# Attention over a cached context: K of some units scored ahead of a row's chain, V alone beside it, twelve chunks a row kept instead of eleven

## The chip, the cores and the metric

The kernel runs on one core of one Trainium2 chip. The metric is the device time of one execution in microseconds; the time before is the median of three runs. PE is the matrix engine, DVE the vector engine, ACT the scalar engine, POOL the general engine; SP's queue issues nearly all transfers.

## The reference

A batch of 8 rows, one token each, goes twice through an attention block and an MLP block. The attention reads the same cache of 4096 positions both times: 8 heads of K and V of 256 elements per row, 2 query heads on each. Cut to what matters:

```python
def _A_ref(x, k_cache, v_cache, wq, wo):          # x: (8, 1, 448)
    q = (x @ wq) as (B, 16 heads, 1, 256)
    scores = einsum("bhqd,bhkd->bhqk", q, k) * 256**-0.5
    o = einsum("bhqk,bhkd->bhqd", softmax(scores), v)
    return o as (B, 1, 4096) @ wo

x = x + _A_ref(_layernorm(x), K, V, wq, wo)
x = x + _B_ref(_layernorm(x), w1, w2, w3, w4)
x = x + _A_ref(_layernorm(x), K, V, wq, wo)
x = x + _B_ref(_layernorm(x), w1, w2, w3, w4)
```

With one token a row the shifted branch of `_B_ref` (w1, w2) adds nothing, since every shifted part is padding. What is left of it is `x + gelu(layernorm(x) @ w3) @ w4`. The cache is 268 MB, and the second pass over it needs a query that depends on the row's whole first pass.

## The kernel before

**Units and chunks.** Work is cut into units (pass, row, pair of heads), 2 x 8 x 4 of them. A unit has 4 chunks of K and 4 of V, each 1 MiB (128 partitions of 8 KB). Chunks live in 15 places in SBUF (`NC`, `slots`). `tasks` is the order of the units, `items` the order of the chunks: K chunk by chunk with V of the unit before between them (`due`). `loads` are the items that are fetched, in the same order; `emit_loads` (L660 to L707) issues a load on SP's queue, at L675 for two neighbouring places at once (2 MiB) and at L700 for one, whenever a place is free in program order. The issue then waits on the chip until the last reader of that place is done.

**K.** `transpose_k` (L713) turns a chunk on DVE in three instructions. `scores` (L728) multiplies it with the spread query `qbd`, 128 columns wide, or 256 wide when two chunks lie in neighbouring places; `paired` says which units are scored two chunks at a time. `exps` (L737) takes the exponential on ACT and its sums. `transpose_p` (L764, L771) turns the unit's p into `ptw`, from which `pv` (L783) multiplies a chunk of V in 16 products into a bank `o`.

**The row's chain.** After the last unit of a row's first pass, a serial chain runs: `half` (normalise and evict one bank, L420 to L467), output projection (`add_cols`, L358), `norm` (L220 to L298, with a power on POOL, L247), `mlp_hidden` (L376, GELU L394 to L399), w4 (L358), `norm` again, `project_q` (L309), which gives the query of the second pass; `spread_q` (L328, L332) lays it out. `chain`, `first_half`, `first_last` and `last` are Python generators. Each `yield` ends a step, and `step` puts steps into the engines' program before and after an item, so many that a given number (`total`) is spread over a given stretch of items. PE runs its program in order, so a step's products stand between the products of the chunks.

**What is kept.** `kept` names the chunks of a row that stay in their places from the first pass to the second: K of pairs 3 and 2, V chunks 1 to 3 of pair 3, 11 in all. `inner`, one more V chunk, is copied to PSUM (`away`, L748) and back (`back`, L755); a quarter of `part` goes to a fifth bank (L960, L978). While a row's chain runs, its 11 kept chunks hold 11 of the 15 places. Beside it stand three units with K and V: one or two of the second pass of the row before, and one or two of the first pass of a later row.

Of the kernel before, what the change touches and what calls it, by code (L numbers as in the profile page):

```python
# [17 lines left out]
def kernel(  # L18
# [42 lines left out]
    NC = 15  # L61

    kept = [(gp, 0, n) for gp in (GP - 1, GP - 2) for n in range(4)]
    kept += [(GP - 1, 1, n) for n in range(1, 4)]
# [45 lines left out]
    ptz = consts.tile([128, 520], BF16, name="ptw")  # L110
    nc.vector.memset(ptz[:], 0.0)
    ptw = ptz[:, 0:512].rearrange("p (a n w) -> p a n w", a=4, w=8)

    misc = psum.tile([128, 512], FP32, name="misc")
    ot_bank = misc[:, 256:320]
# [5 lines left out]
    nc.tensor.matmul(o_both[:], ptz[:, 0:128], ptz[:, 0:512], start=True, stop=True)  # L121

    def room_ps(what, nb):

        at, n = {"y": (320, 8), "st": (336, 2), "h": (352, HC), "q": (384, NB2)}[what]
        if nb == 1:
            return misc[:, at : at + n]
        if nb < Bn:
            at = {"y": 416, "st": 456, "h": 128}[what]
            return misc[:, at : at + n * nb]  # L130
        at, n = {"y": (0, 8), "st": (64, 2), "h": (80, HC), "q": (256, NB2)}[what]
        return store[0][:, at : at + n * nb]
# [40 lines left out]
    qbds = [consts.tile([128, 8, GP, 4, 2], BF16, name=f"qbd{k}") for k in range(3)]  # L173
# [127 lines left out]
    def project_q(b0, nb, qT):  # L301

        yield from norm(xT[:, :, b0 : b0 + nb], nb, False)
        q_ps = room_ps("q", nb).rearrange("p (c b) -> p c b", b=nb)
        for j in range(2):
            for h in range(Hq):
                for fc in range(4):
                    w, xi = wblk(wq_sb, HD, 2 * h + j, fc)
                    nc.tensor.matmul(  # L309
                        q_ps[:, j * Hq + h, :],  # L310
                        w,
                        xbs(nb)[:, xi, :],
                        start=(fc == 0),
                        stop=(fc == 3),
                    )
                if h % 4 == 3:
                    yield
        nc.vector.tensor_copy(qT, q_ps)
        yield
# [49 lines left out]
    def mlp_hidden(b0, nb):  # L369
# [3 lines left out]
        for c in range(HC):  # L373
            for fc in range(4):
                w, xi = wblk(w3_sb, F, c, fc)
                nc.tensor.matmul(  # L376
                    h_ps[:, c * nb : c * nb + nb],
                    w,
                    xbs(nb)[:, xi, :],
                    start=(fc == 0),  # L380
                    stop=(fc == 3),
                )
            if c % 4 == 3:
                yield
        yield
# [24 lines left out]
    def mlp(b0, nb):  # L410
        HT = yield from mlp_hidden(b0, nb)
        yield from out_cols(lambda c: HT[:, c, :], w4_sb, HC, b0, nb, 1)

    def z_cols(zall, gps):
# [15 lines left out]
        z_ps = misc[:, 480 : 480 + 4 * np_].rearrange("p (n g) -> p n g", n=4)  # L430
# [13 lines left out]

    def half(o_ps, zall, g8, OT):


# [7 lines left out]
        )  # L455
        o_sb = chn.tile([128, Dh], FP32, tag="o_sb")
# [4 lines left out]
        ot_ps = ot_bank[:, 32 * g8 : 32 * g8 + 16].rearrange("p (j h) -> p j h", j=2)  # L461
# [5 lines left out]
        nc.vector.tensor_copy(OT[:, :, 8 * g8 : 8 * g8 + 8], ot_ps)  # L467
        yield

    in_use = []  # L470

    def first_half(b, st):

        OT = work.tile([128, 2, Hq, 1], BF16, tag="OT", bufs=1)
        st["OT"] = OT
        yield from half(st["o", 0], st["z"], 0, OT[:, :, :, 0])
        yield from add_cols(
            y_room(1)[:, 0], lambda i: OT[:, i % 2, i // 2], wo_sb, range(NB2 // 2), 1
# [4 lines left out]
    def chain(b, st):  # L483
        OT = st["OT"]
        yield from half(st["o", 1], st["z"], 1, OT[:, :, :, 0])
        yield from add_cols(
            y_room(1)[:, 1], lambda i: OT[:, i % 2, i // 2], wo_sb, range(NB2 // 2, NB2), 1
# [8 lines left out]
    def first_last(b, st):  # L496

        yield from half(st["o", 1], st["z"], 1, OT2[:, :, :, b])
# [14 lines left out]
    def last(b, st):  # L513
        yield from half(st["o", 0], st["z"], 0, OT2[:, :, :, b])
# [13 lines left out]
    tasks = [(0, 0, gp) for gp in free + keep] + [(0, 1, gp) for gp in free]  # L528


    tasks += [(0, 2, free[0])]
    for b in range(Bn):
        tasks += [(1, b, gp) for gp in keep[::-1]]
        if b == Bn - 2:
            tasks += [(0, b + 1, gp) for gp in keep]
            tasks += [(1, Bn - 3, free[-1])] + [(1, b, gp) for gp in free]
        elif b == Bn - 1:
            tasks += [(1, b, gp) for gp in free]
        else:
            early = 0 < b < Bn - 3  # L540
            tasks += [(1, b, free[0])] * early + [(0, b + 1, gp) for gp in keep]
            tasks += [(1, b, gp) for gp in free[early : 1 if b == Bn - 3 else 2]]
            if b + 2 < Bn:
                tasks += [(0, b + 2, gp) for gp in (free[1:] if b == 0 else free)]


    def flushed(n):

        if n + 1 == len(tasks):
            return True  # L550
        ps, _, gp = tasks[n + 1]
        return ps == 1 and gp == keep[-1]


    items, due = [], []
    for n in range(len(tasks)):
        for c in range(4):
            items.append((n, 0, c))
            items += due[:1]
            del due[:1]  # L560
        due += [(n, 1, c) for c in range(4)]
        if flushed(n):
            items += due
            due = []
# [23 lines left out]
    def paired(n, c):  # L588

        ps, _, gp = tasks[n]  # L590
        u = c - c % 2
        if ps == 0:
            return gp in keep
        return all((gp, 0, k) in kept for k in (u, u + 1))

    used_at = {it: k for k, it in enumerate(items)}
    again = {(tasks[n][1:], kv, c): k for k, (n, kv, c) in enumerate(items) if tasks[n][0] == 1}
# [32 lines left out]
    def both_for(it):  # L630
# [3 lines left out]
        if it not in held:  # L634
            if kv or c % 2 or tasks[n][0] or not paired(n, c) or mate not in loads[:3]:
                return None
# [122 lines left out]
    def transpose_p(p_sb):  # L759
# [3 lines left out]
        for t in range(4):  # L763
# [7 lines left out]
        nc.scalar.copy(  # L771
            ptw[:, :, :, 6:8],
            pt_ps.rearrange("p t k (a h) -> p a (t k) h", a=4),
        )

    def pv(o_ps, v, a, gp):


        g = 2 * gp + a // 2
        for y in range(16):  # L780
            q = y % 4
            at = 128 * a + 8 * (4 * q + y // 4) + 6 - 2 * (g % 4)
# [9 lines left out]
    def pv_cols(o_ps, v, a, gp):  # L792

        g = 2 * gp + a // 2
        for y in range(16):
            for j in range(2):
# [3 lines left out]
                    ptw[:, a, 4 * (y % 4) + y // 4, 6:8],  # L800
# [34 lines left out]
    def add_gen(kind, b, g, at, until, total):  # L835
        gens.append({"kind": kind, "b": b, "g": g, "at": at, "until": until, "n": 0, "of": total})

    def step(idx):

        for kind in ("chain", "last", "rest"):  # L840
# [3 lines left out]
            if e["n"] == 0:  # L844
                e["at"] = max(e["at"], idx)
            if e["n"] < e["of"] * (idx - e["at"] + 1) / max(e["until"] - e["at"], 1):
# [4 lines left out]
    def TURN(n):  # L851
        return int(paired(n, 0) and tasks[n][0] == 0)

    first_of = {}
    for idx, (n, kv, c) in enumerate(items):
        first_of.setdefault((tasks[n][:2], kv), idx)
    rz_gp = None

    for idx, it in enumerate(items):
# [9 lines left out]
        if (ps, b, gp, kv, c) == (0, Bn - 1, REST, 0, 0):  # L869
            assert pairs_done[1, MID - 1] == 4  # L870
            add_gen("rest", 0, rest(), idx + 1, idx + 18, 23)
        p = where[(b, gp), (kv, c)] if ps == 1 and (stays(it) or inside(it)) else where[it]
# [3 lines left out]
        if kv == 0:  # L876
# [16 lines left out]
            if "z" not in st:  # L893
                z_t = chn.tile([128, 2, GP], FP32, tag="zall", bufs=3)
# [4 lines left out]
            if not (ps == 1 and stays(it)):  # L899
                transpose_k(slot)  # L900
            step(idx)
            turn = None
            if c == TURN(n) and n - 1 in p_of:
                turn = lambda t=p_of.pop(n - 1): transpose_p(t)
            if not paired(n, c):
                scores(p, c, qbd, gp, between=turn)
            elif c % 2 != ps:
                x = c - c % 2
                two = [p, where[(b, gp), (0, x + 1)] if ps else where[n, 0, x]]
                if not ps:  # L910
                    two.reverse()
# [13 lines left out]
        else:  # L925
            st = state[ps, b]
            if c == 0 and n in p_of:
                transpose_p(p_of.pop(n))
# [3 lines left out]
            if final and gp in free:  # L932
                pv_cols(oc, slot, c, gp)
# [15 lines left out]
            else:  # L949
# [6 lines left out]
                pv(st["o", g8], slot, c, gp)  # L956
# [4 lines left out]
            if c == 3:  # L961
                done = pairs_done[ps, b] = pairs_done.get((ps, b), 0) + 1
                if done == 2 and ps == 0:
                    add_gen("chain", b, first_half(b, st), idx + 1, idx + (16 if b == 0 else 21), 10)
                elif done == 2:
                    add_gen("chain" if final else "last", b, first_last(b, st), idx + 1, idx + 13, 9)
                elif done == 4 and ps == 0:
                    add_gen("chain", b, chain(b, st), idx + 1, first_of[(1, b), 0] - 1, 38)
                elif done == 4 and not final:
                    add_gen("last", b, last(b, st), idx + 1, idx + (7 if b == Bn - 2 else 13), 6)  # L970
        if not (ps == 0 and stays(it)):
            if (ps, gp, kv, c) == (1, keep[-1], 0, 0):
                kept_place = p
            else:
                places.append(p)
        soon = items[idx + 1] if idx + 1 < len(items) else it
# [72 lines left out]
```

## Time and profile before

| what | value |
|---|---|
| median of three runs | 1099.54 us (1097.26 to 1105.74) |
| span of the profiled execution | 1093.6 us |
| PE busy | 674.9 us (62%), 15063 products |
| DVE busy | 599.1 us (55%) |
| ACT busy | 125.9 us (12%) |
| moved by DMA | 446.80 MB, mean 409 GB/s |
| L713, K turned on DVE | 462.0 us, 576 instructions, 858 ns mean |
| L728, scores on PE | 281.9 us, 6720 products |
| L783, p times V on PE | 241.9 us, 3968 products, 387 ns mean |

The span is that of one profiled execution, from its first to its last instruction; the median counts what lies around it too, 5.9 us more here. Products overlap on PE, so a busy time of PE is no measure of its peak. The granted clock is the share of full speed that PE was given in a stretch. A place's "hold" below is the time from a chunk's landing to the issue of the next load into its place.

### The profile page before, as it was taken

What the parts mean: (1) busy time and instruction counts of PE and PEld (TensorE: products, weight loads), DVE (VectorE), ACT (ScalarE), POOL (GpSimd) and SP (SyncE); (2) the same over time, 40 slices, a digit from 0 to 9 for tenths busy, and PEclk for the clock granted to TensorE, in tenths of its full rate; (3) what the DMA queues carried; (4) which work ended last, traced back from release to release, by engine and by line L of the source; (5) the groups of instructions that cost most, each with busy time, mean ns of one, the idle gap of its engine ahead of it and who ended that gap; (6) DMA issues with size and microseconds to landing.
All of it is one profiled execution on the core that took longest, in us unless ns stands there. A gap on an engine that the chain in (4) does not pass through costs nothing. (4 is left out here: it accounts for less than half of the span.)

```text
span 1093.6 us, 32866 instructions
## 1 busy us (share of the span) xinstructions
PE 674.9 (62%) x15063; PEld 451.8 (41%) x15063; DVE 599.1 (55%) x1215; ACT 125.9 (12%) x362; POOL 16.3 (1%) x27
## 2 busy tenths in 40 slices
PE   3234568456864677446774467834776477767775
PEld 2123345334642355324552245522454244545554
DVE  4256564656366555555465564665637553585462
ACT  0001101110110111101021001201111101111110
POOL 0000000000000000000000000000000000000000
PEclk9986556655575556555566555665556555665565
DMA  9999999999999999999999999999999999999994
GB/s 356 394 427 419 416 403 420 420 416 407 418 423 419 406 417 422 423 419 402 419 422 423 420 401 418 423 421 417 411 416 421 420 398 419 421 411 409 421 417 188
DMA packets 62010, 446.80 MB, mean 409 GB/s; under 512 B 6568, under 2 KB 10544, under 8 KB 12336
## 3 DMA queue, kind: packets, MB, share of 16 engines
q1 hardware_dynamic: 61680, 444.32, 98.6%
q8 instruction: 118, 1.93, 0.7%
q10 hardware_dynamic: 192, 0.38, 0.2%
q14 instruction: 20, 0.16, 0.0%
HBM read 444.67 MB, written 0.01 MB: 407 GB/s over the span
## 5 line engine op out<-in xcount | busy, mean ns | idle before, releaser
L713 DVE STREAM_TRANSPOSE places<-places 128x512 uint32<-128x512 uint32 (+1 forms) x576 | 462.0, 858 | 263.1 <-DMA places<-in_A_k_cache_dram 262.7
L728 PE MATMUL sc<-places,qbd 128*8 128x128 bf16 (+1 forms) x6720 | 281.9, 309 | 217.8 <-DVE places L713 179.7
L783 PE MATMUL o<-places,ptw 128*8 128x256 bf16 x3968 | 241.9, 387 | 144.6 <-DMA places<-in_A_v_cache_dram 122.1
L728 PEld LDWEIGHTS <-qbd 128*8 128x8 bf16 x6720 | 161.2, 101 | 312.8 <-issue 136.8
L783 PEld LDWEIGHTS <-ptw 128*8 128x8 bf16 x3968 | 114.1, 109 | 192.2 <-issue 151.0
L737 ACT ACTIVATE p_n<-sc 128x256 bf16<-128x256 f32 x128 | 95.6, 747 | 763.1 <-PE sc L728 763.1
L309 PEld LDWEIGHTS <-wq_sb 128*128 128x128 bf16 x1152 | 36.0, 104 | 28.3 <-issue 18.4
L358 PEld LDWEIGHTS <-wo_sb 128*128 128x128 bf16 x1280 | 38.4, 102 | 19.8 <-issue 19.8
L332 DVE CAST qbd<-misc 32x64 bf16<-32x64 f32 x64 | 13.8, 216 | 55.6 <-PE misc L328 55.0
L309 PE MATMUL misc<-xb,wq_sb 128*128 128x1 bf16 x1024 | 34.5, 166 | 6.2 <-ACT ptw L771 3.2
L358 PE MATMUL misc<-OT,wo_sb 128*128 128x1 bf16 x1024 | 34.5, 165 | 1.2 <-issue 1.2
L737 ACT ACTIVATION_READ_ACCUMULATOR p_n<-sc 128x1 f32 x128 | 33.9, 265 | 0.0
L771 ACT CAST ptw<-misc 128x128 bf16<-128x128 f32 x64 | 17.4, 273 | 139.1 <-PE misc L764 79.1
L463 PEld LDWEIGHTS misc<-R,o_sb 128*128 128x128 f32 x124 | 26.1, 292 | 9.4 <-issue 8.6
L247 POOL TENSOR_TENSOR t<-t,nhalf 128x2 f32<-128x2 f32 (+2 forms) x20 | 14.0, 703 | 1064.9 <-DVE t L268 1064.9
L463 PE MATMUL misc<-R,o_sb 128*128 128x8 f32 x124 | 28.8, 342 | 0.1
L431 PE MATMUL misc<-zm,one 128*128 128x8 f32 (+1 forms) x66 | 18.5, 354 | 15.0 <-DVE zm L423 14.2
L755 DVE STREAM_TRANSPOSE places<-store 128x512 uint32<-128x512 uint32 x32 | 20.1, 684 | 10.7 <-PE sc L728 10.6
L431 PEld LDWEIGHTS misc<-zm,one 128*128 128x128 f32 x66 | 16.0, 300 | 21.5 <-issue 15.8
L376 PEld LDWEIGHTS <-w_sb 128*128 128x128 bf16 x560 | 17.2, 105 | 9.4 <-issue 9.2
L376 PE MATMUL misc<-xb,w_sb 128*128 128x1 bf16 (+1 forms) x560 | 18.5, 166 | 3.6 <-DVE xb L286 2.2
L748 DVE STREAM_TRANSPOSE store<-places 128x512 uint32<-128x512 uint32 x32 | 19.9, 690 | 0.9 <-DMA places<-in_A_v_cache_dram 0.8
(103 smaller groups left out, 241.9 us busy)
## 6 DMA issues: line engine op xcount, KB each, us to landing
places<-in_A_v_cache_dram SPq DMA_DIRECT2D x215, 1024.0 KB, 9.5
places<-in_A_k_cache_dram SPq DMA_DIRECT2D x146, 1024.0 KB, 9.9
places<-in_A_k_cache_dram SPq DMA_DIRECT2D x23, 2048.0 KB, 18.7
places<-in_A_v_cache_dram SPq DMA_DIRECT2D x8, 768.0 KB, 7.2
wo_sb<-in_A_wo_dram SPq DMA_DIRECT2D x1, 3584.0 KB, 27.5
wq_sb<-in_A_wq_dram SPq DMA_DIRECT2D x3, 1024.0 KB, 8.0
w_sb<-in_B_w_dram SPq DMA_DIRECT2D x1, 1568.0 KB
w_sb<-in_B_w_dram SPq DMA_DIRECT2D x3, 448.0 KB, 26.2
```

What stands on the lines that cost most here:

```text
L309: nc.tensor.matmul(q_ps[:, j * Hq + h, :], w, xbs(nb)[:, xi, :], start=(fc == 0), stop=(fc == 3),)
L358: nc.tensor.matmul(y_ps[:, fc, :], w[:, i, at : at + 128], rhs(i), start=start, stop=stop, skip_group_check=open is not None,)
L376: nc.tensor.matmul(h_ps[:, c * nb : c * nb + nb], w, xbs(nb)[:, xi, :], start=(fc == 0), stop=(fc == 3),)
L431: nc.tensor.matmul(z_ps, ones, zm[:], start=True, stop=True)
L463: nc.tensor.matmul(ot_ps[:, j], o_sb[:].rearrange("p (i j) -> p j i", j=2)[:, j], R[:], start=True, stop=True)
L713: nc.vector.transpose(w, w)
L728: nc.tensor.matmul(sc[32 * k : 32 * k + 8, 128 * x : 128 * (x + nx)], qbd[:, ep, gp].rearrange("p a h -> p (a h)"), v, start=(n == 0), sto ...
L737: nc.scalar.activation(p_sb[:, :, :, 2 * u : 2 * u + 2].rearrange("p t i x -> p x t i"), sc[:, 256 * u : 256 * u + 256].rearrange("p (x t ...
L748: nc.vector.transpose(store[n][:].bitcast(U32), slot[:].bitcast(U32)[:, 512 * n : 512 * n + 512])
L755: nc.vector.transpose(slot[:].bitcast(U32)[:, 512 * n : 512 * n + 512], store[n][:].bitcast(U32))
L771: nc.scalar.copy(ptw[:, :, :, 6:8], pt_ps.rearrange("p t k (a h) -> p a (t k) h", a=4),)
L783: nc.tensor.matmul(o_ps[32 * q : 32 * q + 8, :], ptz[:, at : at + 8], v[:, y * Dh : (y + 1) * Dh], start=False, stop=(y >= 12), skip_group ...
```

## The change

One more V chunk a row is kept: chunk 2 of pair 2, 12 in all. The order of the units is new. Between two chains come K and V of the row's second pass and of the next row's kept pairs, and K alone of up to four further units (`ahead`): the two others of the row's second pass, and two of the first pass three rows on. These units' p is kept in one of four slots `psv`. Beside the chain then come only the V chunks of those units: 16, or 8 for the last two rows. For the first row they are four first-pass units. From `psv` ACT copies p chunk by chunk into a ring of two (`ptw`, `spread_p`), one chunk ahead.

K of all these units is scored two chunks at a time, and both places come free after the pair (`late`). The chain's steps are coarser (32 products of wo and wq, 28 of w3 and w4 in a step). Chains no longer follow a total: one step is placed at every call of `step`, and V chunks of scored-ahead units have a third call between the halves of their products. `half` starts its sums before the row's last V chunks (`ready`) and only one may run at a time (`locked`). There are two spread queries instead of three, and rooms in the `misc` bank are moved.

```diff
-    kept += [(GP - 1, 1, n) for n in range(1, 4)]
+    kept += [(GP - 1, 1, n) for n in range(1, 4)] + [(GP - 2, 1, 2)]
-    qbds = [consts.tile([128, 8, GP, 4, 2], BF16, name=f"qbd{k}") for k in range(3)]
+    qbds = [consts.tile([128, 8, GP, 4, 2], BF16, name=f"qbd{k}") for k in range(2)]
...
-                if h % 4 == 3:
+                if h % 8 == 7:
                     yield
...
-            if c % 4 == 3:
+            if c % 7 == 6:
                 yield
-        yield
...
+    ahead = [[(0, 1, gp) for gp in free] + [(0, 2, gp) for gp in free]]
+    for b in range(Bn - 1):
+        units = [(1, b, gp) for gp in free]
+        if b + 3 < Bn:
+            units += [(0, b + 3, gp) for gp in free]
+        ahead.append(units)
+    def block(k, v=None):
+        fresh = [(number[v], 1, c) for c in range(4)] if v else []
+        if k is None:
+            items.extend(due + fresh)
+            due.clear()
+            return
+        number[k] = len(tasks)
+        tasks.append(k)
+        for c in range(4):
+            items.append((number[k], 0, c))
+            items.extend(due[:1])
+            del due[:1]
+            if c == 0:
+                due.extend(fresh)
+    def first_kept(b, units, before):
+        k2, k3 = ((0, b, gp) for gp in keep)
+        todo = list(units)
+        block(todo.pop(0), before)
+        if len(todo) > 2:
+            block(todo.pop(0))
+        block(k2)
+        block(todo.pop(0), k2) if todo else block(None, k2)
+        block(k3)
+        block(todo.pop(0), k3) if todo else block(None, k3)
+        for u in units:
+            block(None, u)
...
     def paired(n, c):
         ps, _, gp = tasks[n]
-        u = c - c % 2
-        if ps == 0:
-            return gp in keep
-        return all((gp, 0, k) in kept for k in (u, u + 1))
+        return gp in keep or tasks[n] in saved
+    def late(it):
+        n, kv, c = it
+        return kv == 0 and paired(n, c) and not (tasks[n][0] == 1 and stays(it))
...
-    def pv(o_ps, v, a, gp):
+    def pv(o_ps, v, a, gp, r, between):
         g = 2 * gp + a // 2
         for y in range(16):
+            if y == 8 and between is not None:
+                between()
...
-            if e["n"] < e["of"] * (idx - e["at"] + 1) / max(e["until"] - e["at"], 1):
+            if not e["of"] or e["n"] < e["of"] * (idx - e["at"] + 1) / max(e["until"] - e["at"], 1):
...
+    def spread_p(it):
+        if it in ring_of or it in plain or it[0] not in slot_of:
+            return
+        ring_of[it] = v_items.index(it) % 2
+        nc.scalar.copy(ptw[:, ring_of[it], :, 6:8], psv[slot_of[it[0]]][:, it[2]])
...
+            spread_p(it)
+            if it in v_next:
+                spread_p(v_next[it])
...
+                calm = tasks[n] in saved
+                pv(st["o", g8], slot, c, gp, ring_of[it], (lambda: step(idx)) if calm else None)
...
-            else:
+            elif not late(it):
                 places.append(p)
+            elif c % 2:
+                places.extend([where[n, 0, c - 1], p])
```

## The prediction

> **What bounds the kernel now.** I read the page's slices of the span first: is any engine short of time, or is it the transfers?
>
> ```profile
> PEclk9986556655575556555566555665556555665565
> DMA  9999999999999999999999999999999999999994
> GB/s 356 394 427 419 416 403 420 420 416 407 418 423 419 406 417 422 423 419 402 419 422 423 420 401 418 423 421 417 411 416 421 420 398 419 421 411 409 421 417 188
> ```
>
> The DMA engines are busy in every slice but the last, while PE has 62% and DVE 55% of the span. The kernel is a stream of 1 MiB chunks of K and V at about 420 GB/s; a chunk takes 1.0486 MB / 421 = 2.49 us. Only two things change its time: fewer bytes, or moments in which the next load is issued too late. So I asked next what SP's queue, which issues every load, waits for.
>
> ```profile
> SPq L700 <- DVE places L713: 203.7, 72, 4.8
> SPq L700 <- PE o L783: 180.0, 128, 9.5
> ```
>
> It waits for places: a chunk of K is given back after its scores, a chunk of V after its 16 products of L783. Then I set a stretch with many free places (the kept chunks just used up) beside a chain, by windows of engine time.
>
> ```profile
> 430.00:490.00 60.00, 29.02 (x602) 17.66 (x594) 35.38 (x53) 6.72 (x19) 0.00 (x0) 0.57 1.01 422
> 490.00:560.00 70.00, 50.77 (x1070) 33.62 (x1071) 36.37 (x88) 8.39 (x25) 1.26 (x2) 0.52 1.01 412
> ```
>
> The last column is GB/s: 422 with many places, 412 beside the chain, where 15 places less 11 kept leave 4. The last but two is the granted PE clock, about 0.5 beside the chain. Then the DMA issues, in three windows: two of one issue each (501.5 to 501.7 and 904.5 to 904.6), then 490 to 560; the last column is the median time from issue to landing.
>
> ```profile
> places<-in_A_k_cache_dram SPq DMA_DIRECT2D x1, 1024.0 KB, 6.9
> ```
>
> ```profile
> places<-in_A_v_cache_dram SPq DMA_DIRECT2D x1, 1024.0 KB, 7.0
> ```
>
> ```profile
> places<-in_A_v_cache_dram SPq DMA_DIRECT2D x14, 1024.0 KB, 7.9
> places<-in_A_k_cache_dram SPq DMA_DIRECT2D x11, 1024.0 KB, 7.0
> ```
>
> A chunk is 2.49 us of transfer, yet takes 6.9 us from issue to landing even when little is queued. I paired every 1 MiB load's issue with its completion in the trace: none is under 6.88 us, and one in ten is under 7.23. Sorted by how long before its predecessor's landing a load was issued: at 5 us or more it lands 2.5 us after it; at 4.0 to 4.5 us (15 loads) 2.68 us after; the one under 4.0 (3.985) 2.95 us after. So a load issued less than about 4.5 us before its predecessor lands comes late.
>
> Last, the timeline at the end of one chain, where V alone is in work, PE's and then SP's rows:
>
> ```profile
> 541.35 1.01 PE L309 MATMUL misc<-xb,wq_sb 128*128 128x1 bf16 x32
> 542.29 1.03 PE L783 MATMUL o<-places,ptw 128*8 128x256 bf16 x16
> 544.22 1.02 PE L783 MATMUL o<-places,ptw 128*8 128x256 bf16 x16 [0.90 <-DMA places<-in_A_v_cache_dram]
> 546.72 1.02 PE L783 MATMUL o<-places,ptw 128*8 128x256 bf16 x16 [1.48 <-DMA places<-in_A_v_cache_dram]
> ```
>
> ```profile
> 543.36 0.33 SPq L700 DMA_DIRECT2D places<-in_A_k_cache_dram  x1
> 545.28 0.33 SPq L700 DMA_DIRECT2D places<-in_A_v_cache_dram  x1
> 547.78 0.33 SPq L700 DMA_DIRECT2D places<-in_A_k_cache_dram  x1
> ```
>
> What SP issues here, K or V, goes into the place that V has just left. V lands every 2.50 us, its products take 1.02 us, and SP issues 0.04 us after them. A place of V is thus held 1.1 us from landing to the next issue when PE is free, and 32 projection products in front cost it 1.0 us more.
>
> **The change, part by part.** The sum starts at the profiled execution: span 1093.6 us. The median of the timed runs is 1099.5, 5.9 us more, which I leave unchanged; differences in the span are added to the median.
>
> *Bytes.* One more chunk a row stays: 8 x 1.0486 = 8.39 MB less, of 446.8. At 422 GB/s: **-19.9 us**; nothing hides a byte here, so this term is sure.
>
> *The other loads.* Before, eight stretches beside chains (120-180, 230-300, 360-430, 490-560, 620-690, 750-820, 870-930, 960-1040; 550 us in all) ran at 409 to 413, about 2.4% under 422: 13 us lost. In the new order K comes in runs, between the chains, when up to 15 places turn over. Between nothing and all 13 is regained; only the last loads before a chain still have few places, so I take **-10 us**.
>
> *V in three places.* Beside each chain come 16 chunks of V for the first six rows and 8 for the last two: 112. Fifteen places less 12 kept are 3. A place goes round in landing time plus hold: 6.95 + 1.1 = 8.05 us, 2.68 us a chunk, against 2.49. That is +0.19 us on 112 chunks, +21 us, with an idle PE. Beside the chain the hold grows. A chunk of a scored-ahead unit gets three steps of the chain: ahead of its products, between their halves, behind them; the steps now hold 28 or 32 matrix products (0.9 and 1.0 us by L358, L376 and L309). After the last V of the row's own unit the chain has 23 steps, so it covers 8 chunks. Laid out one behind the other (eviction and 4 small products 1.4 us, norm 0.85 us to its sum and 2.0 or 1.65 us from sum to vector, GELU 1.2 us), PE gives the chunks back 1.08, 1.62, 1.08, 1.46, 1.98, 1.46, 2.16 and 1.64 us after landing, mean 1.56: output projection runs over into the second, one step of w4 and one of wq splits the fifth and the seventh, the rest run over. Cycle 6.95 + 1.56 = 8.51, 2.84 us a chunk, +0.35. A 16-chunk row loses 8 x 0.35 + 8 x 0.19 = 4.3 us, an 8-chunk row 2.8: 6 x 4.3 + 2 x 2.8 = 31. Landings beside chains were nearer 7.1 than 6.95: +0.05 x 112 = 6. **+37 us**. Ends: +7 if the three places keep the 412 GB/s of the four (280 us x 2.4%); +45 if the later chunks are held like the first eight. I take the value from the landing floor, because V's own rows show it.
>
> The Trainium skill, page "DMA: Bandwidth & Descriptors", section "Anatomy of one DMA", fits a GpSimd-issued transfer with 2.0 us plus bytes over 436 GB/s, an estimate of 4.4 us for this chunk; three places would then turn in 5.5 us, lose nothing, and the sum would be that of the first rival below. No 1 MiB load of this trace, all of them issued by SP, came near 4.4; the smallest was 6.88.
>
> *Out of the V stretch.* The kept K's must be scored before places come back. In the row above the next issues came 3.05 and 5.8 us after 547.78; four places had loads in flight to cover that, three have one chunk less. About 0.5 us twice a row, seven rows: **+6 us** (0 to 8).
>
> *Steps with cover.* p spread per chunk on ACT: 62 units x 4 casts, each between 0.2 and 0.27 us (L397, L771), at most 67 us on an engine busy 126 of 1094, and issued one chunk ahead; uncovered it is 0.3 us of hold. The last scored-ahead unit turns p at its own first V: 0.29 on PE, 0.27 on ACT, hand-offs, about 1 us once a row, within the spread of the hold. A third spread of q a row (0.9 us DVE, about 2.7 with its waits) falls in K's run, where loads are ahead. K runs ten chunks to one of V: 11 x 2.49 = 27.4 us of transfer against 10 x 2.43 (three transposes of L713) + 2.7 = 27.0 us of DVE: just covered; its failure is the third rival. Pairs in one 256-wide scoring (396 ns against 2 x 285) save PE time, off the path. Start and tail: same chunks in the same order, 0.
>
> Sum: -20 - 10 + 37 + 6 = +13, so **1113 us**.
>
> **Rivals.** *Three places are enough* (faster). The trace hardly shows a load issued under 4 us ahead, so 6.9 may be partly queueing and shrink when the queue empties. It decides where the landing falls below 7.47 - 1.1 = 6.4 us. Then V keeps 412: -20 - 13 + 7 = -26, 1073; half of it, 1085. Against it: loads stop at 6.88, and those issued latest came late. *The floor alone* (within 1%): PE's clock rises in the V stretches, products take 0.61 us as at 930 us, and the chain hides; +10 to +21 for V, 0 to +6 behind it: -20 - 10 + 15 + 3 = -12 to -20 - 10 + 21 + 6 = -3, 1088 to 1097; and the forecast short by a few us. For it: PE has less to do. Against: the windows beside the chains show it at 0.50 to 0.56. *K's run bound by DVE or by places that must be neighbours* (slower still): late by 2 to 3 us a row, 7 rows, +18: 1131. For it: 27.0 against 27.4. Against: up to 15 places hold the lag. That 12 chunks were not kept, or that four places turned, I exclude: the listing counts 15 - 12.
>
> **Numbers.** Forecast 0.42 (its own range, by the ends of its terms, -20 - 13 + 31 + 0 to -20 + 0 + 45 + 8: 1098 to 1132; what of it falls under 1110 is counted with the floor case), three enough 0.20, floor alone 0.27, DVE or pairs 0.11. Range: 1084 (half of the first rival) to 1134 (the third); about one in ten beyond each end. Within 1% (1088.5 to 1110.5, about what a measurement can tell): the floor case, 0.27; faster 0.20; slower 0.53.
>
> **What would show it.** Right: about 438.4 MB; in each V stretch GB/s near 370 to 390, three loads in flight, landings near 6.9, V every 2.7 to 3.0 us, PE waiting for V there; 420 between. Wrong: landings below 6.4 us there and 410 GB/s or more (first rival); PE clock near 1 there (second); a dip in K's run with DVE full or SP waiting for a neighbour's place (third). A span whose rate falls elsewhere would make the working wrong altogether.

## The result, and the profile after

The changed kernel takes 1135.84 us (median; 1129.38 to 1138.53) against 1098.4 us for the kernel before on the same chip: ratio 1.031, 95% interval 1.0259 to 1.0362. It is slower, as forecast, but by more: 37 us where 13.5 were predicted, 2 us above the predicted range. The profiled execution spans 1136.7 us, 43.1 more than that of before; it is the slowest of its four, and the accounts below are of it.

The page's slices of the span, after:

```profile
PEclk9985555756556555565555655556555655566565
DMA  9999999999999999899998999999999799999994
GB/s 357 397 424 428 423 392 340 368 425 417 365 365 397 423 396 364 326 427 421 419 337 321 428 423 409 359 356 428 421 402 362 313 423 418 348 424 421 358 396 200
```

Before, the lowest slice between the third and the last was 398 GB/s. Now the rate falls eight times, once a row, to 313 to 365, and is back above 420 between. The bytes did fall:

```profile
DMA packets 56386, 438.25 MB, mean 386 GB/s; under 512 B 5944, under 2 KB 9920, under 8 KB 11712
```

438.25 MB against 446.80. So the kernel moves less and moves it more slowly, in places that repeat. SP's queue, which issues the loads, shows what it waits for (total us, times, longest):

```profile
SPq L738 <- DMA places<-in_A_v_cache_dram: 195.1, 121, 7.0
SPq L738 <- PE o L819: 167.3, 123, 3.8
SPq L738 <- PE sc L766: 153.9, 59, 9.3
```

In the first line a load can't be issued since the V in its place has not landed yet. Before, the same wait took 110 us:

```profile
SPq L700 <- DMA places<-in_A_v_cache_dram: 110.1, 61, 4.7
```

That it has grown points at a ring of places that is too short. I then cut one row (the third) at its own events: from the first V product beside the chain to the last, the 16 us behind that, and the K run that follows. Columns: stretch, length, busy us and count of PE, PEld, DVE, ACT and POOL, granted PE clock, DMA share, GB/s.

```profile
428.09:474.34 46.25, 30.63 (x600) 20.58 (x599) 6.67 (x38) 4.21 (x19) 1.25 (x2) 0.50 0.97 367
474.34:490.34 16.00, 12.56 (x281) 8.74 (x280) 9.25 (x21) 4.12 (x14) 0.00 (x0) 0.50 0.76 307
491.00:564.00 73.00, 35.08 (x712) 19.97 (x701) 57.61 (x87) 12.18 (x44) 0.00 (x0) 0.57 1.01 422
```

Against 422 GB/s the first loses 46.25 x (1 - 367/422) = 6.0 us, the second 4.4 us in a third of the length, the K run nothing. The same cut in all eight rows gives two sums that this text uses for every kernel: **46 us in the V stretches** and **30 us in the exits**. Together 76; all windows of 10 us from 60 us to the tail, summed the same way, lose 77 after and 14 before. The account closes: 77 - 14 less the 20 us of bytes is 43, the difference of the spans. The first line also shows that the DMA engines are hardly idle in the V stretch (share 0.97): the queue is short there rather than empty. Issues paired with landings in the trace give two or three loads in flight nearly all the time there, 2.3 to 2.5 MiB on average in each row's stretch, and the rate is 353 to 380 GB/s all the same.

The two places in detail. PE's rows at the end of that V stretch:

```profile
461.53 1.02 PE L819 MATMUL o<-places,ptw 128*8 128x256 bf16 x16 [1.53 <-DMA places<-in_A_v_cache_dram]
465.01 1.03 PE L819 MATMUL o<-places,ptw 128*8 128x256 bf16 x16 [2.23 <-DMA places<-in_A_v_cache_dram]
467.33 1.03 PE L819 MATMUL o<-places,ptw 128*8 128x256 bf16 x16 [0.77 <-DMA places<-in_A_v_cache_dram]
469.80 1.03 PE L819 MATMUL o<-places,ptw 128*8 128x256 bf16 x16 [1.45 <-DMA places<-in_A_v_cache_dram]
473.32 1.02 PE L819 MATMUL o<-places,ptw 128*8 128x256 bf16 x16 [2.49 <-DMA places<-in_A_v_cache_dram]
```

PE is idle in front of each chunk and waits for the load. Three chunks come in 8.3 us (461.53 to 469.80, 465.01 to 473.32), with every third late by 1 us: three places, each turning in 8.3 to 8.5 us from issue to issue, 7.2 us of it from issue to landing (the five loads issued between 454 and 467 us; it is also the median of the 88 loads of V issued in the eight stretches):

```profile
places<-in_A_v_cache_dram SPq DMA_DIRECT2D x5, 1024.0 KB, 7.2
```

Behind the last of them, all engines but the weight loads:

```profile
475.07 0.88 DVE L339 CAST qbd<-misc 32x64 bf16<-32x64 f32 x4
476.10 0.99 PE L473 MATMUL misc<-R,o_sb 128*128 128x8 f32 x4 [1.66 <-DVE qbd L339]
477.02 1.88 PE L766 MATMUL sc<-places,qbd 128*8 128x256 bf16 x32
478.83 1.86 PE L365 MATMUL misc<-OT,wo_sb 128*128 128x1 bf16 x64
479.02 0.33 SPq L738 DMA_DIRECT2D places<-in_A_k_cache_dram  x1
```

V's last products end at 474.34. The next place comes back only when the first kept pair is scored, and in front of that stand the spread of q on DVE and the other row's half of the attention result (L473), which sits in PE's queue ahead of the scores and itself waits 1.66 us. SP issues at 479.02, 4.7 us after the last V. Its issue before that was at 470.87; that load landed at 477.56 and the one of 479.02 at 483.92. Between the two landings, 6.36 us, lies one chunk where 2.49 would do. In the sixth row it is worse; the 16 us there, and SP's queue:

```profile
885.63:901.63 16.00, 12.56 (x296) 8.80 (x296) 9.37 (x20) 3.99 (x14) 0.00 (x0) 0.54 0.62 245
```

```profile
883.33 9.98 SPq L738 DMA_DIRECT2D places<-in_A_k_cache_dram  x2
```

Two issues in 9.98 us, the second at 892.98, 7.35 us after that row's last V product (885.63); the DMA share is 0.62 and the rate 245 GB/s.

### The profile page after: what moved, and what is told of

It reads as the page before. It is cut to its first block, busy times and chain, and to the rows that moved or that the text cites. A ratio compares the mean times of both kernels' runs of the same rounds, so it can differ in the third digit from the quotient of the medians.

```text
span 1136.7 us, 30536 instructions
## 1 busy us (share of the span) xinstructions
PE 652.4 (57%) x13748; PEld 421.3 (37%) x13748; DVE 605.1 (53%) x1242; ACT 164.0 (14%) x610; POOL 16.3 (1%) x27
## 2 busy tenths in 40 slices
DMA packets 56386, 438.25 MB, mean 386 GB/s; under 512 B 5944, under 2 KB 9920, under 8 KB 11712
## 4 chain that ended last, share of the span: by engine, by line
DMA 54%; PE 23%; DVE 15%; SPq 3%; issue 2%; ACT 1%; POOL 1%; DVEq 0%; ACTq 0%
DMA places<-in_A_v_cache_dram 35%; DMA places<-in_A_k_cache_dram 19%; DVE places L751 11%; PE sc L766 9%; PE o L819 7%; PE misc L365 3%; SPq L174 2%; PE misc L316 2%; DVE store L786 1%; PE misc L473 1%; DVE qbd L339 1%; SPq L738 1%; ACT p_n L775 1%; DMA wq_sb<-in_A_wq_dram 1%; POOL t L254 1%
## 5 line engine op out<-in xcount | busy, mean ns | idle before, releaser
L766 PE MATMUL sc<-places,qbd 128*8 128x128 bf16 (+1 forms) x5376 | 252.2, 339 | 247.0 <-DVE places L751 227.9
L819 PE MATMUL o<-places,ptw 128*8 128x256 bf16 x3968 | 236.8, 384 | 176.9 <-DMA places<-in_A_v_cache_dram 142.3
L766 PEld LDWEIGHTS <-qbd 128*8 128x8 bf16 x5376 | 135.2, 104 | 324.2 <-DVE places L751 163.7
L819 PEld LDWEIGHTS <-ptw 128*8 128x8 bf16 x3968 | 105.8, 104 | 246.1 <-issue 148.3
L900 ACT COPY ptw<-psv 128x32 bf16<-128x32 bf16 x248 | 50.9, 225 | 216.9 <-PE o L819 215.7
L468 DVE MEMSET o<- 128x256 f32 x31 | 8.4, 272 | 96.8 <-ACT o_sb L467 52.6
L440 DVE RECIPROCAL rz<-misc 128x8 f32<-128x8 f32 (+1 forms) x33 | 6.6, 201 | 97.2 <-PE misc L437 82.6
L809 ACT CAST psv<-misc 128x128 bf16<-128x128 f32 x64 | 17.0, 265 | 242.4 <-PE misc L802 239.8
L316 PEld LDWEIGHTS <-wq_sb 128*128 128x128 bf16 x1152 | 33.9, 104 | 26.5 <-issue 16.8
L473 PE MATMUL misc<-R,o_sb 128*128 128x8 f32 x124 | 28.7, 342 | 23.7 <-DVE qbd L339 13.3
L365 PEld LDWEIGHTS <-wo_sb 128*128 128x128 bf16 x1280 | 36.9, 104 | 10.3 <-issue 10.2
L473 PEld LDWEIGHTS misc<-R,o_sb 128*128 128x128 f32 x124 | 26.1, 292 | 33.9 <-ACT o_sb L467 19.9
L316 PE MATMUL misc<-xb,wq_sb 128*128 128x1 bf16 x1024 | 31.9, 166 | 7.0 <-DVE xb L283 6.8
L365 PE MATMUL misc<-OT,wo_sb 128*128 128x1 bf16 x1024 | 29.8, 166 | 0.0
L339 DVE CAST qbd<-misc 32x64 bf16<-32x64 f32 x92 | 19.7, 214 | 16.5 <-PE misc L335 15.6
L467 ACT COPY o_sb<-o 128x256 f32<-128x256 f32 x31 | 11.5, 372 | 95.9 <-PE o L819 95.9
```

The lines of the kernel that those rows point to most:

```text
L316: nc.tensor.matmul(q_ps[:, j * Hq + h, :], w, xbs(nb)[:, xi, :], start=(fc == 0), stop=(fc == 3),)
L339: nc.vector.tensor_copy(qbd[32 * a : 32 * a + 32, :, :, a, :], qs.rearrange("p e (f g u h) -> p (e f) u g h", f=2, u=2, h=2)[:, :, u],)
L365: nc.tensor.matmul(y_ps[:, fc, :], w[:, i, at : at + 128], rhs(i), start=start, stop=stop, skip_group_check=open is not None,)
L473: nc.tensor.matmul(ot_ps[:, j], o_sb[:].rearrange("p (i j) -> p j i", j=2)[:, j], R[:], start=True, stop=True)
L766: nc.tensor.matmul(sc[32 * k : 32 * k + 8, 128 * x : 128 * (x + nx)], qbd[:, ep, gp].rearrange("p a h -> p (a h)"), v, start=(n == 0), sto ...
L819: nc.tensor.matmul(o_ps[32 * q : 32 * q + 8, :], ptz[:, at : at + 8], v[:, y * Dh : (y + 1) * Dh], start=False, stop=(y >= 12), skip_group ...
```

## The experiments

Two explanations stood at the start. *Turn-round*: three places are too few for what a place needs to come round, both in the V stretch and behind it. *PE's order*: the chain's products lie in front of V's and hold places, however many there are. Later experiments take the two sums apart.

### A fourth place

```diff
-    NC = 15
+    NC = 16
...
-    wo_sb = consts.tile([128, NB2, D], BF16, name="wo_sb")
+    wo_sb = consts.tile([128, NB2 // 2, D], BF16, name="wo_sb")
...
-                    w[:, i, at : at + 128],
+                    w[:, i % 16, at : at + 128],
...
-        A_wo.rearrange("(h p j) d -> p h (j d)", p=128, j=2),
+        A_wo[0 : HD // 2].rearrange("(h p j) d -> p h (j d)", p=128, j=2),
```

> The changed kernel with 16 places instead of 15, so 12 chunks stay and 4 turn beside the chain. Room for the place comes from wo: half of it is loaded (1.83 MB less, 4.3 us by 422 GB/s) and used for both halves, so the output projection's values are wrong while its instructions are the same. Theory 'turn-round' (a place's landing plus hold times three is longer than three transfers): the loss in the V stretches falls from 46 us to under 10, the exits from 30 to 8 to 15 because one more load is in flight; 1136 - 55 - 4 = about 1077 (1068 to 1088). Rival 'PE's order' (what holds the places is chain steps and other rows' halves in PE's program, however many places there are): stretches and exits stay within 15 us of the changed kernel, 1117 to 1132.

Measured: 1082.28 us, ratio to the kernel before, as in all that follows, 0.9844 (0.9805 to 0.9884). The third row's stretch and exit:

```profile
406.71:448.02 41.31, 30.41 (x600) 20.64 (x599) 6.67 (x38) 4.22 (x19) 1.25 (x2) 0.50 0.99 393
448.02:464.02 16.00, 12.57 (x244) 7.81 (x244) 9.07 (x19) 3.98 (x13) 0.00 (x0) 0.50 1.00 400
```

PE has the same 600 products for the same 30 us at the same clock of 0.50, and the transfers run at 393 instead of 367, and at 400 instead of 307 behind. Over all rows 3.2 to 3.4 MiB are in flight in the stretches on average, and they lose 13.4 (from 46), the exits 15.9 (from 30), both a little more than was expected of turn-round (under 10, 8 to 15), while the time is inside its range. The order of PE's work was not touched, so that order alone does not cost 46 us: 33 of them, and 14 in the exits, go with one more place. Of the difference, 1136 - 1082 = 54 us, the 1.89 MB less that are loaded (436.36 MB against 438.25; half of wo is 1.84) are 4.5 us at 422 GB/s; the rest is the place.

### The same places by another way, and the two halves of the change

The new order with 11 chunks kept has four places too:

```diff
-    kept += [(GP - 1, 1, n) for n in range(1, 4)] + [(GP - 2, 1, 2)]
+    kept += [(GP - 1, 1, n) for n in range(1, 4)]
```

> The changed kernel with 11 chunks kept instead of 12: 8.39 MB more are loaded (20 us), four places turn in the V stretches. 'Turn-round': stretches under 10 us, exits 8 to 15: 1136 + 20 - 36 - 18 = 1102 (1092 to 1110), so about the kernel before the change. 'PE's order': 1145 to 1156.

Measured: 1106.11 us, 1.0068 (1.0043 to 1.0093); stretches 8.2, exits 15.9: turn-round again. And the old order with 12 kept, the other half of the change:

```diff
-    kept += [(GP - 1, 1, n) for n in range(1, 4)]
+    kept += [(GP - 1, 1, n) for n in range(1, 4)] + [(GP - 2, 1, 2)]
```

> The kernel before the change with its own order, but 12 chunks kept: the twelfth chunk alone, so that K and V of three units pass beside each chain in three places. With the run of the new order and 11 kept (1106, +9) this parts the change in two. 'Turn-round': a K place is held about 3.5 to 4.5 us (2.43 on DVE, then the scores), a V place 1.1 to 2.5; three places with a landing of 6.5 us turn in about 3.1 us a chunk, +0.6 on some 24 chunks a row, 8 rows: +115, less 20 for the bytes: about 1190 (1150 to 1230). If three places cost no more here than in the new order, +40 to +60 - 20: 1115 to 1140.

Measured: 1162.03 us, 1.0571 (1.0523 to 1.0619), inside the range that turn-round gave. Its slices:

```profile
GB/s 355 397 424 422 381 348 393 423 376 344 346 423 422 377 341 394 425 418 347 356 410 419 379 359 339 418 424 394 354 353 423 400 342 354 418 370 370 357 415 181
```

The low stretches are longer than those of after and no deeper: K and V go through the three places beside the whole chain. So the four corners are 1099 (neither), 1106 (order alone), 1162 (twelfth chunk alone), 1136 (both). The twelfth chunk saves 20 us of bytes and takes back those 20 and 63 more in the old order, those 20 and 30 more in the new. The new order does what it is made for, it makes three places less harmful; by itself it gains nothing (7 us slower, with 11 kept in both).

### Less of the chain

The chain's products beside V, most of them left out:

```diff
-                for fc in range(4):
+                for fc in range(4 if nb > 1 else 1):
...
-            y_room(1)[:, 0], lambda i: OT[:, i % 2, i // 2], wo_sb, range(NB2 // 2), 2
+            y_room(1)[:, 0], lambda i: OT[:, i % 2, i // 2], wo_sb, range(1), 2
```

> The changed kernel with most of the chain's matrix products left out: per row one of four products in the query projection and in the first MLP product, and one row block of wo and of w4 instead of 16 and 14, so q, the MLP and the output are wrong; every other instruction, load and wait is there. The V stretches then show the turn-round with the bare hold of 1.1 us. If the holds are made of chain products as the prediction has it, the stretches fall from 46 us to 20 to 28 and the exits lose the 1.86 us of wo products, 30 to about 26: 1108 to 1116. If the landing alone sets the pace, the stretches stay over 38 us: 1124 to 1136. If landing is no limit at all and only PE's products held the places, they fall under 10 us: 1096.

Measured: 1125.37 us, 1.0222 (1.0187 to 1.0256); stretches 33.4, exits 29.2. The third row's stretch:

```profile
421.75:466.45 44.70, 23.99 (x350) 14.02 (x349) 6.65 (x38) 4.21 (x19) 1.25 (x2) 0.50 0.98 378
```

350 products in place of 600, and the rate rises from 367 to 378 only. So about 12.5 of the 46 us are holds behind chain products; 33 stay though PE is busy for only 24 of 44.7 us: 0.30 us for each of the 112 chunks. The forecast had that part at 0.19 (21 us), or 0.24 with its term for longer landings. The 33 us lie between the two cases named (20 to 28, over 38); the time is on the side on which landing alone sets the pace.

### Loads of half the size

```diff
-                nc.sync.dma_start(dst[:, z0:], src[:, z0:])
+                if kv and tasks[t] in saved:
+                    for y in range(2):
+                        nc.sync.dma_start(
+                            dst[:, 8 * Dh * y : 8 * Dh * (y + 1)], src[:, 8 * Dh * y : 8 * Dh * (y + 1)]
+                        )
+                else:
+                    nc.sync.dma_start(dst[:, z0:], src[:, z0:])
```

> The changed kernel, but each V chunk of the units scored ahead is loaded in two transfers of 0.5 MiB, so that the first half of a place is loaded again after the first 8 of V's 16 products. Same bytes, same three places. 'Turn-round': six half places with a landing of about 5.6 us and a hold of about 0.6 us turn in 1.04 us a half, under the 1.25 us of its transfer; the stretches fall from 46 us to under 15 and the exits stay near 30: 1100 to 1110. 'PE's order': PE gives back at the same times, stretches stay over 35 us: 1125 to 1140. If smaller transfers are slower in themselves, the V stretches show under 400 GB/s with three or more half loads in flight all the time.

Measured: 1118.73 us, 1.0182 (1.014 to 1.0223); stretches 26.6, exits 30.1. Both sides missed: the loss fell by 19 us, not to under 15. The third sign was there: 377 to 394 GB/s in the stretches, with three half loads or more in flight all the time until the last 6 us. But whole loads ran at 353 to 380 there, so halves are not shown to be slower in themselves. The DMA issues between 420 and 470 us:

```profile
places<-in_A_v_cache_dram SPq DMA_DIRECT2D x26, 512.0 KB, 6.9
```

The expectation took 5.6 us for the landing of a half; they take 6.9, where the whole chunk took 7.2. All 26 were issued with 2 to 2.5 MiB in front of them, as the whole loads were with 2 MiB, so most of either time is standing in line. What the 19 us came from, earlier products on the first half or the finer queue, was not separated.

### The exit: the chain's steps, the neighbours, both

Two things delay the first places behind V: chain steps and the other row's work between the kept scores, and SP, which issues in order and waits for one certain place (a pair of K needs two neighbours). First, no chain step at the first four kept chunks:

```diff
-            step(idx)
+            if (ps, gp) != (1, keep[-1]):
+                step(idx)
...
-        step(idx)
+        if (ps, gp, kv) != (1, keep[-1], 0):
+            step(idx)
```

> The changed kernel, but no step of any chain or half is placed at the four kept K chunks that are scored first behind a V stretch; the steps come a few chunks later. Takes 0.99 us of products in front of the first kept scoring and 1.86 us between the two away, in eight exits. 'Turn-round': the exit still has only three loads in flight and the first place still comes back about 3 us after the last V; exits fall from 30 us to about 18, 1120 to 1128. 'PE's order': the exit is these products; exits fall to under 8 us, 1110 to 1116.

Measured: 1128.19 us, 1.0273 (1.0231 to 1.0315); exits 23.8 (from 30), stretches 43.0. In the third row the exit runs at 327 instead of 307. That is neither of the two cases (18, under 8): the chain's steps are a part of some 6 us by the profile, while the timed runs (1127 to 1133 us) overlap with those of after. Next, K of the second pass in any place that is free:

```diff
-            if kv or c % 2 or not paired(n, c) or mate not in loads[:3]:
+            if kv or c % 2 or tasks[n][0] or not paired(n, c) or mate not in loads[:3]:
...
-            if kv == 0 and c % 2 == 0 and paired(n, c):
+            if kv == 0 and c % 2 == 0 and paired(n, c) and tasks[n][0] == 0:
```

> The changed kernel, but loads of second-pass K no longer wait for two neighbouring places (neither held nor in one 2 MiB load); they take the first place that is free, and the pair is scored 128 wide where the places are not neighbours. In the exit of one row the changed kernel's next load was issued 7.35 us after the last V, of others 4.7 us, although the first kept place is back after about 3 to 4.5 us. Theory 'neighbour': loads queue behind one that waits for a certain place; exits fall from 30 us to 16 to 22, 1122 to 1128. Theory 'turn-round only': exits stay at 28 to 32, 1132 to 1139.

Measured: 1134.21 us, 1.0284 (1.0232 to 1.0336); exits 24.0, stretches 45.6. The profiled span fell by 5.3 us, and in the sixth row, where SP waited longest, the exit's loss fell from 6.7 to 3.5; the timed runs can't tell the whole from no difference, and 24.0 lies between the two cases (16 to 22, 28 to 32). By the profiles each takes some 6 of the 30 us. Both together, with the fourth place of the first experiment:

> The run with 16 places (12 kept, four turning, half of wo loaded; 1082, exits 16 us) with two of the reliefs: second-pass K takes any free place, and no chain step at the first kept K's. If the rest of the exit is made of these two, the exits fall from 16 to under 6 us: 1071 to 1077. If it is the wait for q and for the kept scoring itself, they stay over 12: 1078 to 1086.

Measured: 1073.18 us, 0.9755 (0.9723 to 0.9787); stretches 11.6, exits 4.7.

```profile
403.94:446.44 42.50, 29.27 (x600) 20.11 (x599) 6.68 (x38) 4.22 (x19) 1.25 (x2) 0.53 1.00 402
446.44:462.44 16.00, 13.50 (x345) 10.26 (x344) 8.94 (x18) 4.17 (x14) 0.00 (x0) 0.54 1.01 418
```

418 GB/s behind the stretch where after had 307, with more PE work in it (345 products against 281). The exit's 30 us are therefore two factors at once: a fourth load in flight takes away 14, and the earlier return of the first kept places 11 of the 16 that are left.

### Ways to live with three places

V of the last two scored-ahead units moved behind the first kept K's, so that both kinds share the three places there (with free places for K):

```diff
-        for u in units:
+        for u in units[:2]:
             block(None, u)
+        due.extend((number[u], 1, c) for u in units[2:] for c in range(4))
```

> As the run without neighbours, and the last two of the four scored-ahead units have their V behind the first kept K's of the second pass, one V chunk after each K chunk, instead of in front of them (six rows; the last two rows have no such units). Three places then turn for 8 chunks a row, not 16, and V covers the exit. 'Turn-round': stretches 46 to about 28 (eight rows of 8 chunks at about 2.9 us, as they run now), exits of the six rows under 2 us each, of the last two about 2.8 each, together 6 to 15: 1136 - 18 - 20 = 1098 (1088 to 1108). If the chain is not ready after 8 chunks and K waits for it, 1108 to 1120.

Measured: 1116.12 us, 1.014 (1.0098 to 1.0183). The alternative named there, that the chain is not ready, held: a dip remained at the end of each shortened stretch, as in this window of 10 us.

```profile
710.00:720.00 10.00, 6.59 (x172) 4.78 (x165) 4.10 (x13) 2.72 (x10) 0.00 (x0) 0.69 0.73 274
```

PE's rows there:

```profile
707.92 1.86 PE L316 MATMUL misc<-xb,wq_sb 128*128 128x1 bf16 x64
712.50 0.99 PE L473 MATMUL misc<-R,o_sb 128*128 128x8 f32 x4 [1.67 <-DVE qbd L339]
713.42 1.02 PE L767 MATMUL sc<-places,qbd 128*8 128x256 bf16 x16
715.41 1.44 PE L820 MATMUL o<-places,ptw 128*8 128x256 bf16 x32
```

K can't be scored (L767) before the chain has made q (L316) and DVE has spread it, and the V that was moved (L820) stands behind that K in PE's order. With halves on top:

> As the run with two units' V behind the kept K, and V of the scored-ahead units in two loads of 0.5 MiB each. 'Turn-round': the 8-chunk stretches go from about 28 to about 18 us: 1088 (1078 to 1098), at or under the kernel before the change. If half loads cost as much as they bring where places are not short, no gain over the run without halves (within 4 us).

Measured: 1115.73 us, 1.0133 (1.01 to 1.0166): nothing more; the expected 1088 was missed, and the other case named there, no gain within 4 us, held.

Last, all reliefs that helped, with the last unit's V alone behind the kept K: once with 12 kept (and halves), once with 11.

> The changed kernel (12 kept, three places) with the same three reliefs of the exit and V of the scored-ahead units in half loads. Half loads alone gave 1119 with 27 us in the stretches and 30 in the exits. Stretches of 12 chunks before the exit: about 21; exits 30 to 8 to 14: 1119 - 6 - 18 = 1095 (1088 to 1106). If the exits stay over 25, over 1110.

Measured: 1106.07 us, 1.0057 (1.0031 to 1.0083); at the upper end of its range; windows from 60 us on lose 48, against 77 after.

> The new order with 11 kept (1106), and the exit relieved three ways: second-pass K takes any free place, no chain step at the first kept K's, and the last of the four scored-ahead units has its V behind the first kept K's, when the chain has ended, one after each K chunk. The exits of that run lost 16 us; six of eight should fall under 1 us, the two of the last rows stay at 2 to 3 each: 1106 - 9 = 1097 (1091 to 1101), level with or a little under the kernel before. If the exits do not move, 1103 to 1109.

Measured: 1097.1 us, 0.9963 (0.9942 to 0.9984); as expected; the windows lose 17. It is the best version that keeps every operand of the computation, 0.4% under the kernel before: hardly anything to gain from the new order at this size. With 12 kept only the kernels with a sixteenth place came clearly under the kernel before, and these load half of wo only and use it twice.

## Why the prediction was wrong

The step that failed is **"Out of the V stretch", +6 us (0 to 8): it measured 30**. The prediction took the next issues behind V from the row above in the trace of before, 3.05 and 5.8 us later, and charged one chunk less in flight with 0.5 us twice a row, in seven rows; all eight lose, 2.7 to 6.7 us each. In the new order what stands in front of the first kept scores is another list (the spread of q, L473 of another row, its projection L365), and the places that come back must suit the load that is next in SP's queue: 4.7 us in the third row, 7.35 in the sixth. It also took the lateness alone for the price. With three loads in flight the queue ran out of work (DMA share 0.76 and 0.62 over 16 us), and a queue that has run empty pays a whole landing again, 4.9 us for the load of 479.02.

Two readings under the sum were wrong as well. There is no floor of 6.88 us for a landing: one load of before was issued at 150.19 us, 2.9 us before its predecessor landed, and DVE began to turn its chunk at 156.48, so it took less than 6.3 us. It came 3.3 us behind its predecessor all the same, late by 0.8.

```profile
150.19 0.33 SPq L700 DMA_DIRECT2D places<-in_A_k_cache_dram  x1
156.48 1.84 DVE L713 STREAM_TRANSPOSE places<-places 128x1024 uint32<-128x1024 uint32 x2 [1.25 <-DMA places<-in_A_k_cache_dram]
```

And the 5.9 us between the span and the median of before are not what lies around a span: every execution on record with its span takes 1.8 to 2.1 us more than it. The rest is spread between executions, and so the spans profiled differ by 43 us where the medians differ by 37.

The other terms, in the prediction's order:

- *Bytes, -20*: right; 438.25 MB, as the forecast's 438.4.
- *The other loads, -10 (0 to -13)*: right; all but about 1 of the 14 us that before lost outside is gone.
- *V in three places, +37 (7 to 45)*: that three places turn too slowly was right, the size a little small: 46 by rate, 42 by the distance of V's products beyond 2.49 us. Its make-up was off: the bare turn-round costs about 33 us (what stayed with the light chain), not 21 + 6, with landings of 7.2 us in the median (5.9 to 8.7) and not 6.95, and chain holds 12.5 instead of 10. The first eight chunks of a row came every 2.95 us (forecast 2.84), the others every 2.75 (2.68).
- *Steps with cover, 0*: nothing of them shows; the K runs hold 420 to 423 GB/s but one at 414.

With the measured terms: -20 - 13 + 46 + 30 = +43, the difference of the spans.

The rivals: *three places are enough* fell with the rate, 353 to 380 GB/s where it needed 412. Its limit of 6.4 us for the landing settled nothing: the median was 7.2, but nine of the 88 loads landed in less. *The floor alone* fell with the granted clock, 0.50 to 0.53 in all eight stretches. *DVE, or places that must be neighbours*: K's run itself was not late, though DVE was busy in 57.6 of its 73 us; but the wait for a neighbour's place came in the exit, where that rival did not look for it, with about 6 us.

The Trainium skill, page "DMA: Bandwidth & Descriptors", section "Anatomy of one DMA", gives an estimate of 4.4 us for one load of 1 MiB, from 2.0 us plus bytes over 436 GB/s for a transfer that GpSimd issues; here SP issues the loads. The runs here show 4.7 to 4.9 us in three loads of after that were issued into an empty queue, so near it, and a median of 7.2 in the V stretches, where others stand in line, so not; the pace of a ring of places was set by the second.

## What to carry to other kernels

A ring of buffers beside a full transfer queue is sized by the whole round, issue to landing in the running stream plus hold: here 7.2 + 1.2 us against 2.49 us a chunk asks for four places, and with three every chunk loses 0.3 us or more. The landing grows with the line, so look at the lead too. An estimate from these numbers: with three places a load is issued 2 x 2.49 - 1.2 = 3.8 us before its predecessor lands, with four 6.3; the table below shows that 4.5 us kept the pace. One buffer given to a cache in SBUF must be paid by the stretch with the fewest buffers, and by the first moment behind it, when no buffer comes back at all: look there for what stands on each queue (PE, DVE and the in-order issue on SP) ahead of the first return. A price taken from the old order's timeline does not hold at a joint that the change lays out anew; write down the new order there instruction by instruction.

## What the runs showed of the hardware that was not expected

How long a load takes depends on when it is issued in relation to the one before. Over the 1491 loads of 1 MiB from SP in the traces of before, after, the fourth place (the first experiment), the new order with 11 kept and the quiet exit, each issue paired with its landing and sorted by how long ahead of its predecessor's landing it was issued (medians, with the smallest and the largest):

```
issued ahead of predecessor's landing   loads  lands behind predecessor   from issue to landing
4.5 us or more                          1247   2.48 us (2.30 to 4.11)     11.4 us (6.97 to 32.9)
3.5 to 4.5 us                            176   2.65 us (2.43 to 4.62)     6.9 us (5.95 to 8.7)
2 to 3.5 us                               52   3.8 us (2.42 to 6.5)       6.8 us (4.85 to 9.6)
under 1.5 us (queue nearly empty)         13   5.1 us (3.35 to 7.5)       4.8 us (4.63 to 6.0)
```

Three more lie between 1.5 and 2 us. The 6.9 us that looked like a floor in the trace of before are mostly a line: 4.4 us until the predecessor lands and 2.49 of the load's own. In the trace of after 45 of 291 loads took less than 6.88 us. One issue of after into the empty queue, at 892.98 us:

```profile
places<-in_A_k_cache_dram SPq DMA_DIRECT2D x1, 1024.0 KB, 4.7
```

The surprise is in the column on the predecessor: a load issued 2 to 3.5 us ahead finds the queue still at work, and yet lands 3.8 us behind its predecessor (median), 1.3 more than its 2.49 us of transfer. Why, and why the values spread so far at the same lead, no run here separated.
